# Zeros late in the plan, routing buffers in an early pool, a fifth half of weights in the place of q and k, twelve raw chunks ahead

## The chip, the core and the metric

The kernel runs on one core of one Trainium2 chip. Its engines are PE (matrix products), DVE (the vector engine), ACT (the scalar engine), POOL (GpSimd) and SP (the engine that here only issues transfers); 16 DMA engines move data between device memory and the on-chip memory. The metric is the device time of one execution in microseconds.

## What is computed

Attention with two kinds of heads, then a mixture of experts in which every expert keeps at most 80 tokens. Shapes: q, k, v are 8 x 8 x 576 x 64; 4608 tokens of 512 features; 8 experts with w1 512 x 1024 and w2 1024 x 512, all float32.

```python
mask_local   = (rel >= 0) & (rel < 32)                   # heads 0 to 3
mask_strided = (rel >= 0) & (key % 32 == query % 32)     # heads 4 to 7
attn = softmax(where(mask, q @ k.T / 8, -1e9)) @ v
x = attn.transpose(0, 2, 1, 3).reshape(4608, 512)
logits = x @ w_gate; expert = argmax(logits); gate_w = max of softmax(logits)
out = zeros
for e in range(8):
    tok = tokens of expert e; if more than 80, the 80 with the largest gate_w
    out[tok] = gate_w[tok] * (relu(x[tok] @ w1[e]) @ w2[e])
```

Of the 4608 rows of the output at most 640 are not zero, so all of it is first written with zeros (18 transfers of 512 KB) and the experts' rows are scattered over them at the end.

## The kernel before

It has three stages.

**The plan** (attention and gates). The operations of eight batches are put into a list (`pn.op`). The class `Plan` gives each of them an engine and a place by a simulation with fixed costs; PE keeps the order in which the list was made, the others take what is ready, the most urgent first. `rank` is a due time and `at` an earliest time in the simulation; a transfer with a rank is only taken there when little is under way. What comes out is only an order for each engine: on the chip each engine runs its list in that order and waits where a semaphore says so. SP's list holds all loads and stores: per batch q and k in two parts each (L402, L404), v in two layouts (`vz`, L413, and `vs`, L424), stores of the attention's rows to `xs` in device memory (L563, L566, L703), and, woven in by `weights()` and `zeros()`, the chunks of weights (L289) and the zeros (L887).

**Weights.** An expert has two halves, w1 and w2; the order of the 16 halves is in `halves` (w1 of expert 0, w1 of 1, w2 of 0, w1 of 2, ...). A half is four chunks of 512 KB. Each chunk is split into two 16-bit parts, `hi` by ACT (L303, in the plan L877 in two pieces) and `lo` by DVE (L304, in the plan L879), and the halves live in eight buffers `spl0` to `spl7`. `NPRE` halves (4 before) are loaded and split within the plan, through two staging buffers (`ring`). Five chunks more are loaded raw in the plan, three right after it: eight raw chunks in `slots`, made of `ring`, `raw` (where q and k land) and `kst` (keys of the strided heads; its other part is the source of the zeros).

**The transition** (L977 on). The last gates are turned; DVE finds the 16 largest of each segment (`max`, `max_index`), counts ranks (L1025, L1037), a product makes the table of tokens (L1064), DVE reads it (`idx`, L1073) and POOL gathers the 80 rows of each of the first four experts from `xs` (`xg`, L1078). The buffers of this stage are in the pool `rt`, which is made after the pool `ap` of the attention is closed, and lies where `ap` lay: the first write of `rt` waits for the last use of what lay there, which includes the last store to `xs` (L703, out of `vz`).

**The experts.** For every half `weave` puts the matrix products, `splits` (as many chunks as `BSPL` says, 3, 3, 4 in turn), `xprep` (turning of the gathered rows, L1124) and `finish` (L1187, scaling and scatter) into one order by the fractions in `WIN`. Each `wsplit` also asks for the load of the chunk eight further on, into the slot that it frees. After down products ACT empties PSUM (`yab`, L947), POOL adds two parts (`y`, L1179), PE turns them (`yt`, L1187).

Names in the profile: `spl<-ring`, `spl<-raw`, `spl<-kst` are splits out of these staging buffers; `out<-kst` is a transfer of zeros; `xs<-vz` the last store of attention rows.

Of the kernel before, what the change touches and what calls it, by code (L numbers as in the profile page):

```python
# [193 lines left out]
def moe_attention(ctx: ExitStack, tc, q, k, v, wg, w1, w2, cap, out):  # L194
    nc = tc.nc
# [71 lines left out]
    halves = [(0, 0)]
# [5 lines left out]
        return spls[h] if h < NPRE else (spls[NPRE:] + spls[:NPRE])[(h - NPRE) % len(spls)]  # L273

    def stage(i):
        i0 = NCH * NPRE
        return ring[i % NR] if i < i0 else slots[(i - i0) % NST]

    def wload(i):

# [8 lines left out]
        nc.sync.dma_start(dst, src)  # L289

    def wsplit(pool=False):

# [4 lines left out]
        hi, lo = s_[:, 0, CH * c:CH * c + CH], s_[:, 1, CH * c:CH * c + CH]
        if pool:
            nc.gpsimd.tensor_scalar(r, r, SC, 0.0, op0=ALU.mult, op1=ALU.add)
            nc.scalar.copy(hi, r)  # L300
            nc.gpsimd.tensor_tensor(lo, r, hi, op=ALU.subtract)
        else:
            nc.scalar.activation(hi, r, AF.Copy, scale=SC)  # L303
            nc.vector.scalar_tensor_tensor(lo, r, SC, hi, op0=ALU.mult, op1=ALU.subtract)  # L304
# [558 lines left out]

    def weights():
        i0 = NCH * NPRE
        for i in range(i0 + 5):
            wk = [("ring", i % NR)] if i < i0 + NR else [rawk[0]] if i == i0 + 2 else \
                ["kst0", "kst1"] + [("qk", 1, 1, m, x) for m in range(2) for x in range(2)]
            t = W0 + WSTEP * i
            add(sy(), lambda e, i=i: wload(i), w=wk, kb=524, at=t, rank=t + 8.0)  # L870
            if i < i0:
                r, s_ = ring[i % NR], spls[i // NCH]
                c = i % NCH
                hi, lo = s_[:, 0, CH * c:CH * c + CH], s_[:, 1, CH * c:CH * c + CH]
                for m in range(WSPL):
                    sl = slice(CH // WSPL * m, CH // WSPL * (m + 1))
                    add(dict(A=ac(CH // WSPL)), lambda e, hi=hi, r=r, sl=sl: nc.scalar.activation(  # L877
                        hi[:, sl], r[:, sl], AF.Copy, scale=SC), r=wk, w=[("hi", i, m)], rank=t + 12.0 + WSTEP)
                    add(dict(V=ve(CH // WSPL)), lambda e, lo=lo, hi=hi, r=r, sl=sl: nc.vector.scalar_tensor_tensor(  # L879
                        lo[:, sl], r[:, sl], SC, hi[:, sl], op0=ALU.mult, op1=ALU.subtract),  # L880
                        r=wk + [("hi", i, m)], rank=t + 13.0 + WSTEP)

    def zeros():
        add(sy(), lambda e: nc.sync.dma_start(xs[0:1], zrow[0][0:1, 0:512]), r=["kst0"], kb=2, slow=5.0, rank=60.0)
        for i in range(18):
# [1 line left out]
            add(sy(), lambda e, i=i, x=x: nc.sync.dma_start(  # L887
                outv[i], zrow[x].unsqueeze(1).broadcast_to([64, 2, 1024])), r=["kst%d" % x], kb=524,
                at=Z0 + ZSTEP * i, rank=Z0 + ZSTEP * i + 15.0)
# [98 lines left out]
    nc.vector.max_index(ci[:, 8:16], cv[:, 8:16], gv2)
# [34 lines left out]
    nc.vector.tensor_scalar(pos.rearrange("p a b -> p (a b)"), cv, 0.0, None, op0=ALU.is_gt)
# [48 lines left out]
    with nc.allow_low_precision("token ids are integers"):  # L1072
        nc.vector.tensor_reduce(idx, tab[:, :, 0:2], op=ALU.add, axis=AX.X)  # L1073
    NX = 4
    xg = [rt.tile([SLOTS, DM], F32, name=f"xg{i}") for i in range(NX)]

    def gather(e):
        nc.gpsimd.indirect_dma_start(out=xg[e % NX], out_offset=None, in_=xs[:, :],  # L1078
# [268 lines left out]
```

## Time and profile before

| | |
|---|---|
| median of 3 runs | 333.69 us (333.15 to 335.94) |
| the profiled execution | 331.08 us |
| its span, first to last instruction | 329.4 us |
| mean granted PE clock | 0.895 |
| busy: PE, DVE, ACT, POOL | 264.4, 227.5, 205.0, 121.0 us |
| moved by DMA | 85.34 MB, 259 GB/s over the span |

The plan runs to about 227 us of the span, the transition to about 247 us, the experts to about 323 us; the rest is the last scatter and the program's end. In the profile's rows "L12" is line 12 of the kernel before, times are microseconds unless marked ns, and the part in brackets at a row's end says how long the engine was idle ahead of it and what ended that. Matrix products are pipelined, so a busy PE need not be at its peak.

### The profile page before, as it was taken

How to read it: one execution, taken by the hardware profiler on the slowest of the kernel's cores; microseconds unless marked ns; L12 is line 12 of the kernel's file. 1: busy time of each engine (PE TensorE's matmuls, PEld its weight loads, DVE VectorE, ACT ScalarE, POOL GpSimd, SP SyncE). 2: the span in 40 equal slices, each digit the busy share in tenths (PEclk: the TensorE clock that was granted, in tenths of full speed). 3: DMA queues.
4: the chain of work that ended last, by engine and by line, in shares of the span. 5: the costliest groups of instructions: out<-in, count | busy, mean ns of one | idle time of the engine just before them, and what ended most of it. 6: DMA issues, size and time to landing. Idle time of an engine off the chain costs nothing. (4 is left out here: it accounts for less than half of the span.)

```text
span 329.4 us, 11542 instructions
## 1 busy us (share of the span) xinstructions
PE 264.4 (80%) x4927; PEld 232.7 (71%) x4927; DVE 227.5 (69%) x443; ACT 205.0 (62%) x325; POOL 121.0 (37%) x148
## 2 busy tenths in 40 slices
PE   5765897989978996996998996967058999699791
PEld 5554786778767795885877785746058999599670
DVE  5882766576952977664686766444757999999920
ACT  1574687569775784673668674352207998999810
POOL 8981384271062353162162270000563152322231
PEclk9997698999997997898799799897676999799987
DMA  7978797999997999999796899953537999999401
GB/s 250 247 224 265 208 354 291 166 400 332 253 278 286 217 243 385 183 254 348 202 325 266 193 319 305 259 153 76 189 107 256 347 372 389 401 401 387 169 23 42
DMA packets 56456, 85.34 MB, mean 259 GB/s; under 512 B 23125, under 2 KB 32341, under 8 KB 56402
## 3 DMA queue, kind: packets, MB, share of 16 engines
q1 hardware_dynamic: 54482, 80.79, 79.5%
q0 software_dynamic: 1920, 3.79, 3.5%
q8 instruction: 40, 0.66, 0.8%
q14 instruction: 14, 0.11, 0.1%
HBM read 63.21 MB, written 20.19 MB: 253 GB/s over the span
## 5 line engine op out<-in xcount | busy, mean ns | idle before, releaser
L419 POOL TENSOR_SCALAR vz<-vz 32x1088 f32<-32x1088 f32 x32 | 36.3, 1136 | 44.2 <-DMA vz<-v 37.8
L1132 PE MATMUL hp<-xe,spl 128*128 128x80 f16 x256 | 32.1, 209 | 0.5 <-ACT xe L1126 0.5
L304 DVE SCALAR_TENSOR_TENSOR spl<-raw,spl 128x1024 f16<-128x1024 f32 x24 | 31.8, 1353 | 0.9 <-ACT spl L303 0.9
L1133 PE MATMUL hp<-xe,spl 128*128 128x80 f16 x256 | 32.0, 209 | 0.3 <-DVE xe L1127 0.3
L1134 PE MATMUL hp<-xe,spl 128*128 128x80 f16 x256 | 32.0, 209 | 0.0
L879 DVE SCALAR_TENSOR_TENSOR spl<-ring,spl 128x512 f16<-128x512 f32 x32 | 26.4, 842 | 7.9 <-ACT spl L877 7.8
L672 PE MATMUL pb<-ptm,vs 72*64 72x72 f32 x512 | 22.4, 257 | 9.7 <-DMA ptm<-ptu 4.4
L532 PE MATMUL pb<-vz,ptl 128*32 128x130 f32 x576 | 25.7, 353 | 4.1 <-ACT ptl L364 4.1
L672 PEld LDWEIGHTS pb<-ptm,vs 72*64 72x64 f32 x512 | 21.0, 162 | 11.0 <-DVE rs L626 3.4
L1133 PEld LDWEIGHTS <-spl 128*128 128x128 f16 x256 | 26.9, 105 | 0.9 <-issue 0.7
L445 POOL TENSOR_SCALAR cp<-raw 128x1152 f32<-128x1152 f32 x13 | 16.1, 1235 | 31.1 <-DMA raw<-k 17.8
L1134 PEld LDWEIGHTS <-spl 128*128 128x128 f16 x256 | 26.8, 105 | 0.4 <-issue 0.4
L1132 PEld LDWEIGHTS <-spl 128*128 128x128 f16 x256 | 26.9, 105 | 0.0
L1169 PE MATMUL yp<-he,spl 128*128 128x160 f16 x224 | 26.9, 243 | 0.0
L532 PEld LDWEIGHTS pb<-vz,ptl 128*32 128x32 f32 x576 | 21.9, 145 | 6.6 <-ACT ptl L364 4.3
L303 ACT ACTIVATE spl<-raw 128x1024 f16<-128x1024 f32 x24 | 24.9, 1055 | 2.5 <-DMA raw<-moe_w 1.9
L1168 PE MATMUL yp<-he,spl 128*128 128x80 f16 x196 | 25.0, 206 | 0.0
L465 PE MATMUL pb<-ident,cp 128*128 128x128 f32 x144 | 20.2, 297 | 5.7 <-DVE cp L445 2.9
L610 PE MATMUL pb<-kst,qs 128*18 128x36 f32 x1024 | 20.0, 252 | 3.4 <-issue 3.4
L465 PEld LDWEIGHTS pb<-ident,cp 128*128 128x128 f32 x144 | 17.3, 151 | 7.2 <-ACT pl L510 3.2
L610 PEld LDWEIGHTS pb<-kst,qs 128*18 128x18 f32 x1024 | 18.3, 122 | 5.7 <-issue 5.7
L364 ACT COPY kst<-pb 64x512 f32<-64x512 f32 (+1 forms) x30 | 21.1, 705 | 1.0 <-DVE kst L366 0.5
(207 smaller groups left out, 708.7 us busy)
## 6 DMA issues: line engine op xcount, KB each, us to landing
ring<-moe_w SPq DMA_DIRECT2D x28, 512.0 KB
raw<-moe_w SPq DMA_DIRECT2D x24, 512.0 KB
raw<-q SPq DMA_DIRECT2D x16, 576.0 KB
raw<-k SPq DMA_DIRECT2D x16, 576.0 KB
out<-kst SPq DMA_DIRECT2D x18, 512.0 KB
kst<-moe_w SPq DMA_DIRECT2D x12, 512.0 KB
vs<-v SPq DMA_DIRECT2D x8, 576.0 KB
vz<-v SPq DMA_DIRECT2D x16, 288.0 KB
```

The costliest lines, as they stand in the source:

```text
L304: nc.vector.scalar_tensor_tensor(lo, r, SC, hi, op0=ALU.mult, op1=ALU.subtract)
L419: nc.gpsimd.tensor_scalar(vz[64 * u:64 * u + 32, h, 1:NTL, u, 0:D], vz[64 * u + 32:64 * u + 64, h, 0:NTL - 1, u, 0:D], 1.0, 0.0, op0=ALU.m ...
L465: nc.tensor.transpose(ps(t, P * (j - a), P * (j - a) + P), src[:, j], ident)
L532: nc.tensor.matmul(ps(t, 512 * k_ + 130 * i, 512 * k_ + 130 * i + 130)[32 * g:32 * g + 32], ptl[:, c, 32 * g:32 * g + 32], vz[:, h, tt, :, ...
L610: nc.tensor.matmul(so[32 * h:32 * h + 18, :, :, z], qs[:, h, r::16], kst[:, :, h, r::16], start=False, stop=(g % 2 == 1 and z == 3), tile_ ...
L672: nc.tensor.matmul(o[64 * x:64 * x + 64, :, h], vs[:, h, 2 * g + x], ptm[:, :, 2 * g + x, h], start=True, stop=True)
L879: add(dict(V=ve(CH // WSPL)), lambda e, lo=lo, hi=hi, r=r, sl=sl: nc.vector.scalar_tensor_tensor(lo[:, sl], r[:, sl], SC, hi[:, sl], op0=A ...
L1132: nc.tensor.matmul(o, w[:, 0, i:i + P], x[:, 0, c], start=first, stop=False)
L1133: nc.tensor.matmul(o, w[:, 0, i:i + P], x[:, 1, c], start=False, stop=False)
L1134: nc.tensor.matmul(o, w[:, 1, i:i + P], x[:, 0, c], start=False, stop=last)
L1168: nc.tensor.matmul(ab[:, 0], w[:, 1, i:i + P], he[:, 0, c], start=False, stop=False)
L1169: nc.tensor.matmul(ab, w[:, 0, i:i + P], he[:, :, c], start=(c == 0), stop=(c == 7))
```

## The change

Four things are changed together, and the numbers of the plan with them.

- **Zeros.** Their earliest time goes from `26 + 8 i` to `150 + 1.5 i` and their due time from 15 to 200 behind that; the plan then puts them late and behind the weights.
- **Routing buffers.** `pl`, `pr`, `ptl` and `ptu` move from the pool `ap` into a pool `ae` ahead of it. `rt` therefore lies over `ae`; the gathered rows `xg` get a pool `rt2` of their own behind it, and `scr` is one row instead of eight.
- **A fifth half.** `NPRE` is 5. The fifth half's buffer is part of a new tile `eb`, in which the attention's `qt`, `qs` and `ktl` also lie; so its four chunks (16 to 19) are split once the last scores have been read.
- **Twelve raw chunks.** Behind the 20 split chunks, 12 are loaded raw: four into `ring` and `raw`, four into the last buffer of halves (`far_`, free until half 7), four more into `raw` and `kst`. From then on a split asks again for the chunk eight further on.

In the experts 44 chunks are split instead of 48; `RS` moves one split ahead of the first `xprep`, `BSPL` spreads the rest over more halves, and `finish` comes a little later.

```diff
-NPRE = 4
-NPOST = 4
+NPRE = 5
+NPOST = 3
...
-    slots = (ring + [raw[:, 0:CH]] + [kstt[:, CH * j:CH * j + CH] for j in range(2)] +
-             [raw[:, CH * j:CH * j + CH] for j in range(1, 4)])
+    slots = ring + [raw[:, CH * j:CH * j + CH] for j in range(4)] + [kstt[:, CH * j:CH * j + CH] for j in range(2)]
...
-    spls = [wpool.tile([P, 2, HALF], F16, name=f"spl{i}") for i in range(NPRE)]
+    eb = wpool.tile([P, 8 * S + 128], F32, name="eb")
+    spls = [wpool.tile([P, 2, HALF], F16, name=f"spl{i}") for i in range(NPRE - 1)]
+    spls.append(eb[:, 0:HALF].bitcast(F16).rearrange("p (a f) -> p a f", a=2))
...
     def stage(i):
-        i0 = NCH * NPRE
-        return ring[i % NR] if i < i0 else slots[(i - i0) % NST]
+        k = i - NCH * NPRE
+        if k < 0:
+            return ring[i % NR]
+        if 4 <= k < 8:
+            return far_[k - 4]
+        return slots[k if k < 4 else (k - 8 + 4) % NST if k < 12 else (k - 12) % NST]
...
-        j = i + (NR if i < NCH * NPRE else NST)
-        if j < NCHUNKS:
+        k = i - NCH * NPRE
+        j = i + (12 if k < 4 else NST)
+        if j < NCHUNKS and not 4 <= k < 8:
             late.append(lambda: wload(j))
...
+    ae = actx.enter_context(tc.tile_pool(name="ae", bufs=1))
     ap = actx.enter_context(tc.tile_pool(name="ap", bufs=1))
...
-    pl = ap.tile([P, 9, P], F32, name="pl")
+    qt = eb[:, 0:2 * S].rearrange("p (h s) -> p h s", h=2)
+    qs = eb[:, 2 * S:4 * S].rearrange("p (h s) -> p h s", h=4)
+    ktl = eb[:, 4 * S:8 * S + 128].rearrange("p (h u s) -> p h u s", h=2, u=2)
+    pl = ae.tile([P, 9, P], F32, name="pl")
...
     flush()
-    for j in range(NR + 3, NST):
-        wload(NCH * NPRE + j)
+    wload(NCH * NPRE + 9)
     warm(WARM_[0])
     actx.close()
     rt = wctx.enter_context(tc.tile_pool(name="rt", bufs=1))
+    rt2 = wctx.enter_context(tc.tile_pool(name="rt2", bufs=1))
     wpool3 = wctx.enter_context(tc.tile_pool(name="wpool3", bufs=1))
     spls += [wpool3.tile([P, 2, HALF], F16, name=f"spl{i}") for i in range(NPRE, NPRE + NPOST)]
+    fl = spls[-1].rearrange("p a f -> p (a f)").bitcast(F32)
+    far_ += [fl[:, CH * j:CH * j + CH] for j in range(4)]
+    for j in list(range(4, 8)) + [10, 11]:
+        wload(NCH * NPRE + j)
...
-    xg = [rt.tile([SLOTS, DM], F32, name=f"xg{i}") for i in range(NX)]
+    xg = [rt2.tile([SLOTS, DM], F32, name=f"xg{i}") for i in range(NX)]
...
-Z0 = 26.0
-ZSTEP = 8.0
+Z0 = 150.0
+ZSTEP = 1.5
+ZR = 200.0
-BSPL = [3, 3, 4]
+BSPL = [3, 2, 3, 3]
-RS = 1
+RS = 2
```

What the plan makes of the new numbers on SP, from the last but one store of the strided heads' rows on (L703 before, L711 now). Before:

```order
L703 DMA xs<-xn 576x1x256
L424 DMA vs<-v 72x4x512
L289 DMA kst<-moe_w 128x2x512
L563 DMA xs<-xl 128x4x256
L566 DMA xs<-xl 64x256
L289 DMA kst<-moe_w 128x1024
L703 DMA xs<-xn 576x1x256
L703 DMA xs<-vz 576x1x256
L289 DMA raw<-moe_w 128x1024 x3
```

And of the changed kernel, where `spl_3152` is the last buffer of halves, used as staging:

```order
L574 DMA xs<-xl 64x256
L295 DMA raw<-moe_w 128x1024
L711 DMA xs<-xn 576x1x256
L898 DMA out<-kst 128x1x1024
L295 DMA raw<-moe_w 128x1024
L295 DMA ring_122<-moe_w 128x1024
L295 DMA ring_123<-moe_w 128x1024
L898 DMA out<-kst 128x1x1024
L295 DMA raw<-moe_w 128x1024
L711 DMA xs<-vz 576x1x256
L898 DMA out<-kst 128x1x1024 x6
L295 DMA raw<-moe_w 128x1024
```

Six transfers now stand between the last two stores to `xs`, where there was none, and behind `xs<-vz` come six zeros and then seven chunks (the one shown, four into `spl_3152` and two into `kst`) instead of three. Ten more zeros stand a batch or two earlier, four and six in a row.

On DVE, the end of the plan, around the logits of the last batch (`lg`), before:

```order
L758 RECIPROCAL mm<-mm 96x6
L759 TENSOR_TENSOR gates<-eq,mm 96x48
L735 TENSOR_REDUCE lg<-pb 96x48
L743 TENSOR_REDUCE mm<-lg 96x6
L744 TENSOR_TENSOR ex<-lg,mm 96x48
L749 TENSOR_TENSOR eq<-lg,mm 96x48
```

And now:

```order
L767 TENSOR_TENSOR gates<-eq,mm 96x48
L890 SCALAR_TENSOR_TENSOR eb<-ring_122,eb 128x512 x2
L743 TENSOR_REDUCE lg<-pb 96x48
L890 SCALAR_TENSOR_TENSOR eb<-ring_123,eb 128x512
L751 TENSOR_REDUCE mm<-lg 96x6
L752 TENSOR_TENSOR ex<-lg,mm 96x48
L890 SCALAR_TENSOR_TENSOR eb<-ring_123,eb 128x512
L757 TENSOR_TENSOR eq<-lg,mm 96x48
```

Four half splits of chunks 18 and 19 have come among the steps of the last gates; four others, of chunks 16 and 17, stand a little ahead. On ACT their four `hi` parts stand the same way around the emptying of the last logits.

The first write of a routing buffer on DVE, with the semaphores that it waits for (DMAHW are those of SP's transfers, DMASW those of POOL's), before:

```order
L979 MAX msk<-msk 128x8 [waits DVE_49]
L982 TENSOR_TENSOR wgt<-msk,segm 128x256 [waits DVE_49]
L987 MAX_INDEX msk<-msk,g_117 128x8
L988 MAX_INDEX msk<-msk 128x8
L1023 TENSOR_SCALAR pos<-msk 128x16 [waits DMAHW0_49,DMASW7_49,DMAHW1_49,DMASW6_49,DMAHW2_49,DMASW5_49,DMAHW3_49,DMASW4_49,DMAHW4_49,DMASW2_49,DMAHW5_49,DMASW1_49,DMAHW6_49,DMASW0_49,DMAHW7_49,Activation_49,Pool_49]
```

And now:

```order
L990 MAX msk<-msk 128x8 [waits DVE_49]
L993 TENSOR_TENSOR wgt<-msk,segm 128x256 [waits DVE_49]
L998 MAX_INDEX msk<-msk,g_117 128x8
L999 MAX_INDEX msk<-msk 128x8
L1038 TENSOR_SCALAR pos<-msk 128x16 [waits DMASW4_49,DMASW5_49,DMASW2_49,DMASW6_49,DMASW1_49,DMASW7_49,DMASW0_49,Pool_49]
```

The wait for SP's transfers, the last store among them, has left this row; what is left are POOL's transfers of `ptm`, whose last user is a batch earlier. The first gather and the first split in `spl5` now wait for SP's stores to `xs` instead.

More of the change, by code (lines that the diff above doesn't have):

```diff
@@ L326, in moe_attention @@
     cps = [ap.tile([P, 9, P], F32, name=f"cp{i}") for i in range(2)]
-    qt = ap.tile([P, 2, S], F32, name="qt")
-    qs = ap.tile([P, 4, S // 2], F32, name="qs")
-    ktl = ap.tile([P, 2, 2, 32 + S], F32, name="ktl")
-    pl = ap.tile([P, 9, P], F32, name="pl")
-    pr = ap.tile([P, 8, 18, 4], F32, name="pr")
-    ptl = ap.tile([P, 9, P], F32, name="ptl")
-    ptu = ap.tile([72, 8, 4, 18], F32, name="ptu")
+    qt = eb[:, 0:2 * S].rearrange("p (h s) -> p h s", h=2)
+    qs = eb[:, 2 * S:4 * S].rearrange("p (h s) -> p h s", h=4)
+    ktl = eb[:, 4 * S:8 * S + 128].rearrange("p (h u s) -> p h u s", h=2, u=2)
+    pl = ae.tile([P, 9, P], F32, name="pl")
+    pr = ae.tile([P, 8, 18, 4], F32, name="pr")
+    ptl = ae.tile([P, 9, P], F32, name="ptl")
+    ptu = ae.tile([72, 8, 4, 18], F32, name="ptu")
     ptm = ap.tile([72, 4, 8, 4, 18], F32, name="ptm")
@@ L865, in weights @@
         i0 = NCH * NPRE
[L866 to L869, printed above, removed]
+        eb_ = [("qk", g, w, m, x) for g in range(2) for w in range(2) for m in range(2) for x in range(w + 1)]
+        add(dict(V=0.01), lambda e: None, w=eb_ + ["eb"])
+        places = [[("ring", 0)], [("ring", 1)], [rawk[0]], [rawk[0], rawk[1]], [rawk[1], rawk[2]]]
+        for i in list(range(i0 + 4)) + [i0 + 8]:
+            wk = [("ring", i % NR)] if i < i0 else places[i - i0 if i < i0 + 4 else 4]
+            t = W0 + WSTEP * i if i < i0 + 4 else W0 + WSTEP * (i0 + 4)
             add(sy(), lambda e, i=i: wload(i), w=wk, kb=524, at=t, rank=t + 8.0)
@@ L874, in weights @@
                 hi, lo = s_[:, 0, CH * c:CH * c + CH], s_[:, 1, CH * c:CH * c + CH]
+                ek = ["eb"] if i >= NCH * (NPRE - 1) else []
                 for m in range(WSPL):
@@ L877, in weights @@
                     add(dict(A=ac(CH // WSPL)), lambda e, hi=hi, r=r, sl=sl: nc.scalar.activation(
-                        hi[:, sl], r[:, sl], AF.Copy, scale=SC), r=wk, w=[("hi", i, m)], rank=t + 12.0 + WSTEP)
+                        hi[:, sl], r[:, sl], AF.Copy, scale=SC), r=wk + ek, w=[("hi", i, m)], rank=t + 12.0 + WSTEP)
                     add(dict(V=ve(CH // WSPL)), lambda e, lo=lo, hi=hi, r=r, sl=sl: nc.vector.scalar_tensor_tensor(
                         lo[:, sl], r[:, sl], SC, hi[:, sl], op0=ALU.mult, op1=ALU.subtract),
-                        r=wk + [("hi", i, m)], rank=t + 13.0 + WSTEP)
+                        r=wk + ek + [("hi", i, m)], rank=t + 13.0 + WSTEP)
     def zeros():
@@ L888, in zeros @@
                 outv[i], zrow[x].unsqueeze(1).broadcast_to([64, 2, 1024])), r=["kst%d" % x], kb=524,
-                at=Z0 + ZSTEP * i, rank=Z0 + ZSTEP * i + 15.0)
+                at=Z0 + ZSTEP * i, rank=Z0 + ZSTEP * i + ZR)
     load(0, 0, 0)
@@ L1017, in moe_attention @@
                      esel.unsqueeze(1).unsqueeze(3).broadcast_to([P, NCAND, E, 5]), op=ALU.mult)
-    scr = rt.tile([P, 8, NSEG * NCAND], BF16, name="scr")
+    scr = rt.tile([P, NSEG * NCAND], BF16, name="scr")
     rank = rt.tile([P, 8], F32, name="rank")
@@ L1024, in moe_attention @@
     for m in range(3):
-        nc.vector.tensor_scalar(scr[:, m], call, cv[:, 4 * m + 3:4 * m + 4], None, op0=ALU.is_gt, op1=ALU.add,
+        nc.vector.tensor_scalar(scr, call, cv[:, 4 * m + 3:4 * m + 4], None, op0=ALU.is_gt, op1=ALU.add,
                                 accum_out=rank[:, m:m + 1])
@@ L1036, in moe_attention @@
     for m in range(4):
-        nc.vector.tensor_scalar(scr[:, 3 + m], call, thr[:, m:m + 1], None, op0=ALU.is_gt, op1=ALU.add,
+        nc.vector.tensor_scalar(scr, call, thr[:, m:m + 1], None, op0=ALU.is_gt, op1=ALU.add,
                                 accum_out=rank[:, 3 + m:4 + m])
@@ L1308 @@
 W0 = 14.0
-WSTEP = 8.5
+WSTEP = 8.0
 WSPL = 2
-Z0 = 26.0
-ZSTEP = 8.0
+Z0 = 150.0
+ZSTEP = 1.5
+ZR = 200.0
 BPOOL = []
-BSPL = [3, 3, 4]
+BSPL = [3, 2, 3, 3]
 WARM = 40
 WARM_ = [48, 0, 32, 0]
-RS = 1
+RS = 2
 EV = dict(y="a", ys="a")
-WIN = dict(b=(0.2, 1), bx=(0.12, 0.55), bf=(0.78, 0.92), bl=(0.3, 0.4))
+WIN = dict(b=(0.2, 1), bx=(0.12, 0.55), bf=(0.8, 0.94), bl=(0.3, 0.4))
 FILL = dict(l=0, s=0, q=0, r=0)
```

1 line of the change is left out of this document (added).

## The prediction

> **What bounds the kernel now.** I first cut the execution into stages: busy time of each engine, granted clock, DMA share and GB/s.
>
> ```profile
> span 329.4 us, 11542 instructions
> 80.00:155.00 75.00, 63.91 (x1284) 55.72 (x1280) 50.02 (x110) 49.70 (x84) 27.89 (x31) 0.93 1.00 273
> 155.00:205.00 50.00, 44.24 (x886) 37.85 (x884) 34.71 (x77) 33.14 (x59) 16.28 (x18) 0.90 0.89 270
> 205.00:227.00 22.00, 17.79 (x256) 14.15 (x252) 11.22 (x44) 9.77 (x19) 0.00 (x0) 0.84 0.57 166
> 227.00:247.00 20.00, 7.49 (x97) 6.96 (x95) 11.36 (x42) 2.00 (x2) 9.20 (x17) 0.73 0.50 152
> 247.00:323.00 76.00, 68.53 (x1300) 64.72 (x1298) 66.23 (x70) 61.75 (x85) 21.84 (x19) 0.91 0.82 300
> ```
>
> The columns are PE, PE weight load, DVE, ACT, POOL. The middle of the plan has DMA full (1.00) and PE with holes; from 205 us DMA is half idle, and in the transition everything is. In the experts PE and DVE are both near 90%, so there it must be asked who waits for whom.
>
> The transition by its timeline (start, duration, engine, idle before):
>
> ```profile
> 226.27 0.45 DVE L988 FIND_INDEX8 msk<-msk 128x8 uint32<-128x288 f32 x1
> 226.79 0.58 SPq L703 DMA_DIRECT2D xs<-vz  x1
> 231.73 2.00 ACT L303 ACTIVATE spl<-ring 128x1024 f16<-128x1024 f32 x2 [5.00 <-DMA xs<-vz]
> 231.89 0.17 DVE L1023 TENSOR_SCALAR pos<-msk 128x16 f32<-128x16 f32 x1 [5.16 <-DMA raw<-moe_w]
> 240.68 0.17 DVE L1073 TENSOR_REDUCE idx<-pb 80x8 int32<-80x16 f32 x1 [0.82 <-PE pb L1064]
> 241.14 1.82 POOL L1078 DMA_INDIRECT xg<-xs,idx  x1 [4.08 <-DVE idx L1073]
> 246.68 0.63 PE L1124 MATMUL xp<-ident,xg 80*128 80x80 f32 x3 [2.89 <-DMA xg<-xs,idx]
> ```
>
> DVE has its indices at 226.72 and may write the first routing buffer only at 231.89. The row blames `raw<-moe_w`, but the buffer lay where `vz` was, and ACT, with the same wait, names the store `xs<-vz`: 4.94 us from its issue to ACT's release. Everything to the first turning at 246.68 hangs on it.
>
> The experts: DVE's groups in 247 to 323, PE's total wait there, and the chain of one such wait.
>
> ```profile
> L304 DVE SCALAR_TENSOR_TENSOR spl<-raw,spl 128x1024 f16<-128x1024 f32 x24 | 31.8, 1353 | 0.9 <-ACT spl L303 0.9
> L304 DVE SCALAR_TENSOR_TENSOR spl<-kst,spl 128x1024 f16<-128x1024 f32 x12 | 14.2, 1211 | 0.0
> L304 DVE SCALAR_TENSOR_TENSOR spl<-ring,spl 128x1024 f16<-128x1024 f32 x10 | 12.5, 1277 | 0.0
> PE yt L1187 <- POOL y L1179: 6.4, 4, 3.2
> 280.36 1.06 ACT L303 ACTIVATE spl<-raw 128x1024 f16<-128x1024 f32 x1 [0.29 <-DMA raw<-moe_w]
> 281.32 0.67 ACT L947 COPY yab<-yp 128x640 f32<-128x640 f32 x1
> 282.07 1.75 POOL L1179 TENSOR_TENSOR y<-yab 128x320 f32<-128x320 f32 x1 [4.23 <-ACT yab L947]
> 283.88 0.89 PE L1187 MATMUL yt<-ident,y 128*80 128x128 f32 x4 [3.21 <-POOL y L1179]
> 247.00:255.00 8.00, 7.18 (x120) 6.87 (x119) 6.07 (x8) 6.32 (x10) 2.72 (x3) 0.60 0.79 255
> 284.00:287.50 3.50, 3.50 (x38) 3.42 (x38) 3.50 (x5) 3.25 (x5) 1.07 (x1) 0.52 1.03 395
> 309.00:311.40 2.40, 0.34 (x3) 0.34 (x4) 2.40 (x3) 2.17 (x4) 1.04 (x1) 1.00 0.02 7
> 311.40:314.80 3.40, 3.40 (x39) 3.33 (x38) 3.40 (x5) 1.12 (x2) 1.20 (x1) 0.50 0.08 22
> ```
>
> ACT, late with its splits, empties `yab` late, POOL adds late, and PE stands 3.21 us; after that its clock is 0.52 for 3.5 us. The same comes again around 311, and the stage begins at 0.60. So the experts run at the pace of the splits, on DVE (66.23 of 76) and behind it ACT and DMA; PE pays for their lag twice, in the gap and in the clock.
>
> The Trainium skill, "TensorE: Matmul & The Clock Gate", section "Why this matters for your kernels", warns of PE gaps above about 3 us; here 2.4 us before 311.4 was enough for a clock of 0.50, by the rule that window would run at full clock and 1.7 us less be to gain. I count every such gap with its clock.
>
> **The change, part by part.** All against the profiled execution, 331.08 us, which is 2.6 us below the median of 333.69; I add that at the end.
>
> *Routing buffers: -5.2.* The first routing write loses the wait for SP's transfers, so 5.16 us go. What is late next is the gather, which needs `xs<-vz` landed, and `idx`. Today the store is released at 231.73 and `idx` would come at 240.68 - 5.16 = 235.5, so 3.8 us of room are left for a store delayed by the transfers now ahead of it. Two zeros and four chunks are put between the last two stores: 6 x 0.524 = 3.1 MB, about 8 us at the 395 GB/s above, where DMA is 0.57 busy in 22 us and so idle for 9.5. I take the room as enough.
>
> *The gather itself: +1.* Now it runs beside six zeros and seven chunks.
>
> ```profile
> DMA to landing us min/median/max: 4.6/5.6/7.7
> ```
>
> These are the eight gathers of today, those amid full DMA among them. The first took 246.68 - 241.14 = 5.5. From 0 to +2.2; I take +1.
>
> *The fifth half: +1.6.* Eight half splits on DVE and eight on ACT join the end of the plan.
>
> ```profile
> L879 DVE SCALAR_TENSOR_TENSOR spl<-ring,spl 128x512 f16<-128x512 f32 x2 | 1.4, 681 | 0.0
> 209.72 0.18 DVE L541 TENSOR_SCALAR rs<-pb 128x18 f32<-128x18 f32 x1 [6.20 <-PE pb L532]
> 219.59 0.40 ACT L364 COPY raw<-pb 128x288 f32<-128x288 f32 x1 [0.87 <-PE pb L718]
> 220.65 0.35 DVE L735 TENSOR_REDUCE lg<-pb 96x48 f32<-96x192 f32 x1 [3.72 <-PE pb L730]
> ```
>
> The first four on DVE (2.7 us) lie in its hole of 6.20 us. Two of the last four lie in the hole of 3.72; the other two stand between the steps of the last gates and cost 2 x 0.68. Ahead of `raw` ACT has 0.87 us for two pieces of some 0.5 each (half of the two whole splits in 2.00 above), +0.2. Sum 1.6; from 0.7 to 5 if the load of chunk 18 or 19 is late, since ACT and DVE then stand before the last logits and PE waits for those.
>
> *Zeros out of the early plan: -3.* Of the 18 zeros only those of the first row below are issued in 155 to 205 today, so eleven leave the time before that, 5.8 MB, of which two more chunks take back 1.0. At the 273 GB/s of the stage that is 17 us of DMA time where DMA is full. What PE would gain is bounded by its gaps there:
>
> ```profile
> out<-kst SPq DMA_DIRECT2D x7, 512.0 KB
> POOL vz L419 <- DMA vz<-v: 37.8, 6, 12.1
> 100.14 0.34 PE L610 MATMUL pb<-kst,qs 128*18 128x36 f32 x8 [3.37 <-issue]
> 128.27 0.99 PE L672 MATMUL pb<-ptm,vs 72*64 72x72 f32 x12 [3.26 <-DVE rs L626]
> ```
>
> If the clock follows as it does in the experts, some 5 us per gap. POOL's 12.1 us for one load of v shows the queue; but neither PE row names DMA. From 0 to -12; I take -3. The late part pays: 18 zeros instead of 7 fall behind 155 us, but eight of them into idle DMA behind 213 us. I count this at 0 to +6, and take 0.
>
> *What a zero costs: as much as a chunk.* A zero is read from 64 partitions. Three zeros and two chunks, issued in turn,
>
> ```profile
> 166.37 0.68 SPq L887 DMA_DIRECT2D out<-kst  x1
> 170.05 1.11 SPq L887 DMA_DIRECT2D out<-kst  x1
> 171.00:177.40 6.40, 6.34 (x163) 5.69 (x162) 4.62 (x14) 5.71 (x11) 3.17 (x5) 1.00 1.04 409
> ```
>
> moved at 409 GB/s; 5 x 0.524 MB take 6.4 us at that, 1.3 each. No row shows several zeros alone, which could be slower; that is rival A. The Trainium skill speaks for A: "SBUF — State Buffer", sections "Door 1: The DMA port swizzle" and "Can I just issue two DMAs to hit both halves?", gives a transfer of 64 partitions half of the ports, 196 GB/s, and hardly any overlap to two on opposite halves, by which a zero would take an estimated 2.7 us. For zeros among chunks the row disagrees.
>
> *The experts: -8.* DVE loses five of the 46 splits behind the first turning (four chunks are split earlier, one moves ahead of it): 5 x 1.21 = 6.1, leaving some 60 of its 66.23. PE's own need:
>
> ```profile
> 265.39 0.53 PE L1187 MATMUL yt<-ident,y 128*80 128x128 f32 x3 [0.35 <-POOL y L1179]
> 272.96 0.50 PE L1187 MATMUL yt<-ident,y 128*80 128x128 f32 x3
> 321.73 1.03 PE L1158 MATMUL yt<-spl,he 128*80 128x512 f16 x4
> ```
>
> One expert without a gap takes 272.96 - 265.39 = 7.57. From 246.68 to 322.76 it has 76.1 us; the two gaps (3.2, 2.4) and half of the two slow windows (1.7 each) make 9.0, and the 3.2 lost at 0.60 in the first 8 us stay. So PE needs about 67 and DVE about 62 with its start: at best -9, at worst, if the splits stay the pace and only their sum shrinks, -6, or -4 if late chunks go on holding ACT up (the 0.29 above). DMA follows: twelve raw chunks are there or on the way at the start, and 32 at 0.524 MB and 395 GB/s need 42 us. I take -8 (-4 to -9).
>
> Sum: -5.2 + 1 + 1.6 - 3 + 0 - 8 = -13.6; 331.08 - 13.6 = 317.5, and on the scale of the median **320 us**.
>
> **Rivals.**
>
> *A: zeros in a row cost double*, because their 64 partitions keep half of the DMA engines idle when no chunk runs beside them: 2.6 us each. Six take 16 us instead of 8, so the seven chunks behind `xs<-vz` and the gather's rows come some 8 us later; about half is hidden behind the transition and the four chunks already there: +5, and the late plan +3. 328. For it: its zeros stand in rows of four and six; against it: the 409 GB/s. 0.18.
>
> *B: the late plan stalls, slower.* DMA is the bound behind 155 us, and loads of v for the last two batches stand behind four and six zeros in SP's one queue. Nine transfers more by balance there: 4.7 MB at the 270 GB/s of that stage, 17 us, all paid; the experts stay at DMA's pace; only the routing gains: 333.7 + 17 + 1.6 - 5.2 = 347. It decides where a load of v lands over 10 us behind its issue, near the 12.1 above. Against it: DMA is 0.57 in 205 to 227, which takes half, giving some 339. 0.07.
>
> *C: the early plan gains in full:* the two gaps and their clocks go, and shorter waits with them, -12 instead of -3: 311. For it: 1.00 of DMA there. Against: no PE row names DMA. 0.12.
>
> *D: one of the parts does nothing* (the gap behind `y` stays, or the gather eats the routing's gain): 326. 0.08.
>
> **The numbers.** Forecast 0.55, on its own 315 to 328: the terms' likelier bounds are +-3 on the plan, +-1 on the gather, -1 and +4 on the experts. 1% (3.3 us) is what a measurement of this kernel can tell. Below 330.4: 0.54 of the forecast, C, 0.07 of D and 0.11 of A: 0.84. Within 1%: 0.07 of A and 0.01 of each of the forecast, D and B: 0.10. Slower: 0.06. The range reaches from C to A: 311 to 330.
>
> **What would show it.** The first routing write within 0.5 us of the last index search; the first turning about 5 us earlier against the plan's end; the eight `eb` splits without long waits; DMA near 0.9 or less in 80 to 155, and near 1 from 205 on; no PE gap above 1 us behind `y`, and a clock of 1.00 through the experts. I am wrong if ACT or DVE wait for `ring` before the last logits, if PE's gaps behind 155 us grow, or if the gather lands over 8 us behind its issue.

## The result, and the profile after

The changed kernel takes 322.80 us (median of 4 runs, 320.56 to 325.84) against 334.81 (4 runs, 333.15 to 337.67): a ratio of 0.961, 95% interval 0.950 to 0.972. The profiled execution fell from 331.08 to 323.60 us, its span from 329.4 to 321.9. The stages of the changed kernel, with the columns PE, PE weight load, DVE, ACT, POOL, clock, DMA share, GB/s:

```profile
80.00:155.00 75.00, 66.31 (x1291) 56.05 (x1288) 50.42 (x112) 49.26 (x85) 25.23 (x29) 0.91 0.91 245
227.00:247.00 20.00, 10.18 (x130) 9.35 (x129) 13.19 (x44) 4.33 (x5) 9.19 (x12) 0.76 1.01 310
243.20:314.10 70.90, 65.41 (x1300) 61.10 (x1300) 61.08 (x65) 56.12 (x80) 22.92 (x18) 0.97 0.89 315
```

DMA fell from 1.00 to 0.91 in the early plan and rose from 0.50 to 1.01 in the transition. The last row is the experts, from the first turning to the last `ys`: 70.9 us at a clock of 0.97, where they had 76.1 at 0.91. The transition by its timeline:

```profile
225.66 0.45 DVE L999 FIND_INDEX8 msk<-msk 128x8 uint32<-128x288 f32 x1
226.03 0.15 DVE L1038 TENSOR_SCALAR pos<-msk 128x16 f32<-128x16 f32 x1
227.17 10.03 SPq L898 DMA_DIRECT2D out<-kst  x6
231.81 2.00 ACT L309 ACTIVATE spl<-ring 128x1024 f16<-128x1024 f32 x2 [5.69 <-DMA xs<-vz]
235.29 2.13 POOL L1093 DMA_INDIRECT xg<-xs,idx  x1 [4.99 <-DMA out<-kst]
243.23 0.77 PE L1139 MATMUL xp<-ident,xg 80*128 80x80 f32 x4 [5.21 <-DMA xg<-xs,idx]
248.76 1.06 ACT L309 ACTIVATE spl<-spl 128x1024 f16<-128x1024 f32 x1 [3.34 <-DMA spl<-moe_w]
```

The first routing write follows the last index search at once (it stood 5.16 us). The gather is issued 5.85 us earlier but takes 7.94 us to the first turning instead of 5.54. Behind that ACT stands 3.34 us for a far chunk (`spl<-moe_w`), which was loaded behind the six zeros that SP issued for 10 us.

All profiled executions of the study, cut at the same places (us; "last search" is the start of the second index search, "to write" the time from there to the first routing write, "gather" from its issue to the first turning, "experts" from that to the last `ys`). The ratios leave out executions more than 1.5% above the fastest of their kernel; where the column is empty, too few are left.

| kernel | profiled | last search | to write | gather | experts | ratio to before, 95% |
|---|---|---|---|---|---|---|
| before | 331.08 | 226.27 | 5.62 | 5.54 | 76.16 | 1 |
| before, again | 335.64 | 230.65 | 5.63 | 5.31 | 75.13 | |
| before, routing buffers alone | 330.50 | 232.40 | 0.36 | 5.66 | 74.73 | |
| after | 323.60 | 225.66 | 0.37 | 7.94 | 70.84 | 0.961 (0.950 to 0.972) |
| after, again | 323.08 | 225.45 | 0.37 | 6.36 | 73.25 | |
| routing over the plan | 328.23 | 225.36 | 7.38 | 8.72 | 68.21 | 0.990 (0.983 to 0.996) |
| zeros early | 322.27 | 226.74 | 0.37 | 8.51 | 68.39 | 0.969 (0.958 to 0.980) |
| zeros behind the far chunks | 320.63 | 223.83 | 0.37 | 9.18 | 69.59 | 0.965 (0.956 to 0.974) |
| old weave | 329.27 | 225.89 | 0.37 | 6.10 | 79.66 | 0.988 (0.972 to 1.004) |
| zeros early, old weave | 327.48 | 226.50 | 0.37 | 8.48 | 74.74 | 0.975 (0.964 to 0.986) |
| the same, four halves | 326.84 | 225.15 | 0.37 | 8.08 | 75.55 | 0.986 (0.977 to 0.994) |
| four halves, new weave | 343.08 | 231.96 | 0.37 | 9.50 | 83.79 | 1.021 (1.005 to 1.038) |
| zeros early, kst first | 324.12 | 229.43 | 0.37 | 8.43 | 67.42 | 0.965 (0.958 to 0.973) |
| six early, kst first | 320.50 | 225.90 | 0.37 | 8.81 | 67.28 | 0.968 (0.961 to 0.975) |

One kernel's plan ends up to 4.4 us apart in two executions (226.27 and 230.65), and an interval is 0.6 to 1.6% to either side; what follows is read stage by stage, and a difference of totals below 1% is not read at all. The mean of the two profiled executions of each kernel: plan 228.5 to 225.6, -2.9; first write -5.25; gather +1.7; experts 75.65 to 72.05, -3.6; the rest under 0.2. Sum -10.0, as 333.36 to 323.34.

### The profile page after: what moved, and what is told of

Read it like the earlier page. It is cut to its first block, busy times and chain, and to the rows that moved or that the text cites. A ratio compares the mean times of both kernels' runs of the same rounds, so it can differ in the third digit from the quotient of the medians.

```text
span 321.9 us, 11566 instructions
## 1 busy us (share of the span) xinstructions
PE 263.3 (82%) x4927; PEld 229.4 (71%) x4927; DVE 228.0 (71%) x449; ACT 203.5 (63%) x328; POOL 121.0 (38%) x147
## 3 DMA queue, kind: packets, MB, share of 16 engines
HBM read 63.21 MB, written 20.19 MB: 259 GB/s over the span
## 5 line engine op out<-in xcount | busy, mean ns | idle before, releaser
L372 ACT COPY eb<-pb 128x640 f32<-128x640 f32 (+3 forms) x52 | 36.1, 729 | 31.0 <-PE pb L473 27.8
L1148 PE MATMUL hp<-xe,spl 128*128 128x80 f16 x256 | 30.6, 205 | 1.4 <-DVE xe L1142 1.4
L1147 PE MATMUL hp<-xe,spl 128*128 128x80 f16 x256 | 30.8, 205 | 0.6 <-ACT xe L1141 0.5
L890 DVE SCALAR_TENSOR_TENSOR spl<-ring,spl 128x512 f16<-128x512 f32 x32 | 24.6, 798 | 9.1 <-ACT spl L888 9.0
L1149 PE MATMUL hp<-xe,spl 128*128 128x80 f16 x256 | 30.6, 205 | 0.5 <-DVE spl L310 0.5
L1149 PEld LDWEIGHTS <-spl 128*128 128x128 f16 x256 | 26.0, 102 | 2.3 <-issue 1.7
L1148 PEld LDWEIGHTS <-spl 128*128 128x128 f16 x256 | 26.0, 102 | 0.9 <-issue 0.9
L1147 PEld LDWEIGHTS <-spl 128*128 128x128 f16 x256 | 26.0, 102 | 0.0
L540 PEld LDWEIGHTS pb<-vz,ptl 128*32 128x32 f32 x576 | 20.5, 137 | 5.4 <-ACT ptl L372 3.5
L310 DVE SCALAR_TENSOR_TENSOR spl<-raw,spl 128x1024 f16<-128x1024 f32 x18 | 23.4, 1327 | 0.5 <-ACT spl L309 0.5
L888 ACT ACTIVATE spl<-ring 128x512 f16<-128x512 f32 x32 | 18.2, 621 | 8.4 <-DMA ring<-moe_w 8.4
L500 PE MATMUL pb<-eb 128*32 128x128 f32 x576 | 20.7, 307 | 1.3 <-ACT eb L372 1.3
L500 PEld LDWEIGHTS pb<-eb 128*32 128x32 f32 x576 | 18.5, 124 | 4.4 <-issue 2.5
L618 PE MATMUL pb<-kst,eb 128*18 128x36 f32 x1024 | 20.0, 251 | 1.6 <-issue 1.6
```

Of the source, the lines that this page charges most:

```text
L372: nc.scalar.copy(o, i)
L500: nc.tensor.matmul(ps(t, P * c, P * c + P)[32 * g:32 * g + 32], qt[:, h, 32 * tt:32 * tt + 32], ktl[:, h, :, 32 * tt:32 * tt + 64], start= ...
L540: nc.tensor.matmul(ps(t, 512 * k_ + 130 * i, 512 * k_ + 130 * i + 130)[32 * g:32 * g + 32], ptl[:, c, 32 * g:32 * g + 32], vz[:, h, tt, :, ...
L618: nc.tensor.matmul(so[32 * h:32 * h + 18, :, :, z], qs[:, h, r::16], kst[:, :, h, r::16], start=False, stop=(g % 2 == 1 and z == 3), tile_ ...
L1147: nc.tensor.matmul(o, w[:, 0, i:i + P], x[:, 0, c], start=first, stop=False)
L1148: nc.tensor.matmul(o, w[:, 0, i:i + P], x[:, 1, c], start=False, stop=False)
```

## The experiments

**The two kernels again.** Nothing is edited.

> The changed kernel once more beside the other runs of this chip, as the measure for them: about 0.96 of the kernel before by every theory.

> The kernel before, profiled a second time, since its first profiled execution (331.08 us) lay below all its others and the changed kernel's did not. Theory, the terms are differences of stages and repeat: last index search at 226 us, 14.4 us from it to the store's release, idx and the first turning at 20 behind it, experts 76 us. Rival, the first execution was a lucky one in a stage whose part I then mis-sized: a stage (the experts with their gaps behind y, or the plan) is 3 to 5 us longer.

The changed kernel, measured together with the two runs on the zeros and with `routing over the plan`: median 325.99 (4 runs, 319.68 to 329.26), 323.08 profiled; the kernel before there 336.08 (14 runs). The kernel before, second profile:

```profile
230.65 0.45 DVE L988 FIND_INDEX8 msk<-msk 128x8 uint32<-128x288 f32 x1
236.28 0.17 DVE L1023 TENSOR_SCALAR pos<-msk 128x16 f32<-128x16 f32 x1 [5.18 <-DMA raw<-moe_w]
250.84 0.77 PE L1124 MATMUL xp<-ident,xg 80*128 80x80 f32 x4 [2.92 <-DMA xg<-xs,idx]
```

From the last search to the first turning 20.19 us, the first time 20.41; the experts 75.1 and 76.2. What differs is the plan, by 4.4 us. So the first profiled execution was low by its plan, and the stages behind it repeat to about 1 us.

**The routing buffers, alone and taken back.** In the kernel before, the early pool `ae` for `pl`, `pr`, `ptl`, `ptu`, the pool `rt2` for `xg` and one row of `scr`; in the changed kernel, the order of the two early pools turned round:

```
-    ae = actx.enter_context(tc.tile_pool(name="ae", bufs=1))
     ap = actx.enter_context(tc.tile_pool(name="ap", bufs=1))
+    ae = actx.enter_context(tc.tile_pool(name="ae", bufs=1))
```

> The kernel before with the routing buffers' part of the change alone: pl, pr, ptl and ptu in an early pool of their own, xg in a second late pool, one row of scr. Theory (term of -5.2): the first routing write comes within 0.5 us of the last index search, the first turning 5 us earlier, and as the experts run at the pace of the splits, the splits' start must move with it: between 3 and 5 us less than before. Rival, the experts are held by the chunks, whatever the time of the first turning: the stage grows by what the routing saves, and the time falls by under 1.5 us.

> The changed kernel with the two early pools in the old order, so that the routing buffers lie over vz again; all else as changed, the six zeros behind the last store too. Theory (term of -5.2): the first routing write waits again until SP's store of vz has landed, some 5.5 us behind the last index search, and the time is 5 us longer than the changed kernel's. Rival: the wait was only exchanged for a longer gather (7.9 us instead of 5.5) and for late chunks, so that with a later gather both come back: the first turning is only some 2.5 us later and the time 1 to 3 us longer. Rival that the plan's end sets it: no difference.

The timeline of the first, and then of the second:

```profile
232.40 0.45 DVE L989 FIND_INDEX8 msk<-msk 128x8 uint32<-128x288 f32 x1
232.76 0.15 DVE L1025 TENSOR_SCALAR pos<-msk 128x16 f32<-128x16 f32 x1
247.44 0.77 PE L1126 MATMUL xp<-ident,xg 80*128 80x80 f32 x4 [3.04 <-DMA xg<-xs,idx]
```

```profile
225.36 0.45 DVE L999 FIND_INDEX8 msk<-msk 128x8 uint32<-128x288 f32 x1
232.74 0.17 DVE L1038 TENSOR_SCALAR pos<-msk 128x16 f32<-128x16 f32 x1 [6.92 <-DMA out<-kst]
250.76 0.77 PE L1139 MATMUL xp<-ident,xg 80*128 80x80 f32 x4 [6.29 <-DMA xg<-xs,idx]
```

Alone, the stretch from the last search to the first turning falls from 20.2 to 15.04 us, the experts do not grow (74.73), and the profiled time is 5.1 us below that of the second profile of before, though the plan ended 1.75 us later. (Its ten timed runs lie between 323.82 and 337.44, median 333.18 against 335.38, too far apart for an interval; what it is worth in the total is therefore open, and the stages alone are read.) Taken back, the wait is there again at 6.92 us, longer than before: the store, with six zeros behind it, now takes 6.76 us from its issue to ACT's release (4.94 before); the first turning comes 7.5 us later than in the first profile of the changed kernel, the experts are 2.6 us shorter, since the far chunks are there by then (ACT waits 0.5 us for chunks), and the profiled time is 4.6 us longer; the ratio is 0.990 (0.983 to 0.996) where the changed kernel has 0.961 (0.950 to 0.972). The term of -5.2 stands, and the rival by which the stage behind eats it falls for the kernel before; for the changed kernel it was right in part.

**The zeros.** Early again (Z0 = 26, ZSTEP = 8, ZR = 15); and twelve in the plan, the last six in the code behind the far chunks:

```
-    for j in list(range(4, 8)) + [10, 11]:
+    for j in range(4, 8):
+        wload(NCH * NPRE + j)
+    for i in range(12, 18):
+        nc.sync.dma_start(outv[i], zrow[i % 2].unsqueeze(1).broadcast_to([64, 2, 1024]))
+    for j in (10, 11):
         wload(NCH * NPRE + j)
```

> The changed kernel with the old due times of the 18 zeros (26, step 8, urgency 15): they stand in the plan up to about 200 us and none behind the last store. Theory (terms -3 and 0): DMA is full again in 80 to 155 us and the plan ends about 3 us later, while the gather lands in 5.5 us instead of 7.9 and the chunks behind it wait for no zeros, 2 to 4 us back: within 2 us of the changed kernel. Rival, the zeros' move carries the gain: 5 us longer or more. Rival, the zeros do harm where they are now and nothing early: 3 us shorter, with the plan's end where it is.

> The changed kernel with the six zeros that stand between the last store and the far chunks issued behind the four far chunks instead, ahead of the two into kst. Theory, the chunks stand behind the zeros (a piece of rival A): ACT's and DVE's waits for the far chunks at 249 to 256 us (3.3 and 2.3 on ACT, 3.2 and 1.8 on DVE) go, the experts are 3 us shorter, and the gather stays at some 8 us. Rival, the zeros only move: the chunks into kst come 8 us later and ACT waits for those: no difference. Rival, the late chunks are the price of the whole DMA being full, whoever stands ahead: waits spread over later chunks, within 1 us.

ACT's largest row of waits for chunks in the experts (in total, how many, the longest), first in the changed kernel, then with the zeros early, then behind the far chunks:

```profile
ACT spl L309 <- DMA spl<-moe_w: 6.1, 3, 3.3
```

```profile
ACT spl L309 <- DMA raw<-moe_w: 1.0, 2, 0.8
```

```profile
ACT spl L309 <- DMA raw<-moe_w: 0.4, 2, 0.2
```

The experts with the zeros early as one window, and the gather and first turning there; then the first turning with the zeros behind:

```profile
244.90:313.30 68.40, 65.78 (x1300) 61.94 (x1300) 61.48 (x65) 56.24 (x80) 21.96 (x18) 0.95 0.76 270
```

```profile
236.37 2.06 POOL L1093 DMA_INDIRECT xg<-xs,idx  x1 [4.99 <-DVE idx L1088]
244.88 0.77 PE L1139 MATMUL xp<-ident,xg 80*128 80x80 f32 x4 [5.98 <-DMA xg<-xs,idx]
```

```profile
242.49 0.77 PE L1143 MATMUL xp<-ident,xg 80*128 80x80 f32 x4 [6.28 <-DMA xg<-xs,idx]
```

In neither is there a wait for `spl<-moe_w`, the far chunks, any more, and the experts then need 68.4 and 69.6 us. So the six zeros cost the stage 1 to 5 us (70.8 and 73.3 less these; in the second profile of the changed kernel the row is 7.0 us), a piece of rival A that the forecast had not priced. Both totals are the changed kernel's within the interval: with the zeros early the plan's end came later (226.74, 226.50 and 229.43 in the three executions with five halves and all zeros early, 227.6 in the mean, against 225.2 in the five with late zeros, 223.83 to 225.89); with the zeros behind, no kernel of the study has a lower median (320.95 of 4 runs), but nothing shows it to beat the changed one. And the gather did not get faster without zeros ahead of it: 8.5 and 9.2 us.

**The weave.** The old numbers in the changed kernel, and the same with the zeros early:

```
-BSPL = [3, 2, 3, 3]
+BSPL = [3, 3, 4]
-RS = 2
+RS = 1
-WIN = dict(b=(0.2, 1), bx=(0.12, 0.55), bf=(0.8, 0.94), bl=(0.3, 0.4))
+WIN = dict(b=(0.2, 1), bx=(0.12, 0.55), bf=(0.78, 0.92), bl=(0.3, 0.4))
```

> The changed kernel with the old numbers of the weave (splits of an expert in groups of 3, 3, 4, one split behind the routing instead of two, the old place of the last group). Theory: a stall of PE behind y of 1 to 3 us comes back in some experts with its slow clock, 0 to 3 us longer. Rival, the splits behind the first turning are what counts and one more of them there costs 1.2 us and no more. Rival that they do nothing: within 0.5 us.

> The changed kernel with the zeros at their old due times and the old numbers of the weave. With the zeros early, no far chunk was late (experts 68.4 us); with the old weave and the zeros late, PE stood 4.61 us behind y at 267.7 us and the experts took 79.7. Theory, the old weave asks for chunks faster than they come, whoever stands ahead of them, and ACT's queue holds y up: a stall behind y and experts of 74 us or more. Rival, the stall came of the late chunks behind the zeros alone: no gap above 1 us, experts 68 to 70 us.

The experts of the first as one window and the 3.5 us behind their longest stall, and that stall by the timeline; then the second's stage and stall:

```profile
241.40:321.00 79.60, 68.88 (x1300) 64.78 (x1300) 60.00 (x66) 57.68 (x80) 25.52 (x19) 0.91 0.82 288
267.70:271.20 3.50, 3.50 (x35) 3.37 (x36) 1.89 (x3) 2.40 (x4) 2.88 (x2) 0.50 1.02 372
```

```profile
261.15 2.35 DVE L310 SCALAR_TENSOR_TENSOR spl<-kst,spl 128x1024 f16<-128x1024 f32 x2
263.42 2.35 DVE L310 SCALAR_TENSOR_TENSOR spl<-ring,spl 128x1024 f16<-128x1024 f32 x2
263.63 4.00 POOL L1194 TENSOR_TENSOR y<-yab 128x320 f32<-128x320 f32 x1 [8.77 <-ACT yab L958]
265.69 1.22 DVE L310 SCALAR_TENSOR_TENSOR spl<-raw,spl 128x1024 f16<-128x1024 f32 x1
266.83 0.48 DVE L1142 SCALAR_TENSOR_TENSOR xe<-xp,xe 128x320 f16<-128x320 f32 x1
267.69 1.07 PE L1202 MATMUL yt<-ident,y 128*80 128x128 f32 x4 [4.61 <-POOL y L1194]
```

```profile
244.50:319.20 74.70, 68.33 (x1300) 64.79 (x1300) 60.72 (x66) 57.73 (x80) 23.93 (x18) 0.90 0.70 248
```

```profile
280.52 3.47 POOL L1194 TENSOR_TENSOR y<-yab 128x320 f32<-128x320 f32 x1 [4.92 <-ACT yab L958]
284.05 1.07 PE L1202 MATMUL yt<-ident,y 128*80 128x128 f32 x4 [5.47 <-POOL y L1194]
```

PE's waits for `y` over the experts (in total, how many, the longest), with the zeros late: the new weave, then the old one. With the zeros early: the new weave; the old one has there the one stall just shown, and the second row is the 3.5 us behind it.

```profile
PE yt L1202 <- POOL y L1194: 1.3, 2, 0.9
PE yt L1202 <- POOL y L1194: 7.4, 4, 4.6
```

```profile
PE yt L1202 <- POOL y L1194: 0.6, 1, 0.6
284.00:287.50 3.50, 3.45 (x34) 3.31 (x35) 1.88 (x3) 2.34 (x4) 0.92 (x1) 0.50 1.03 410
```

The stall behind `y` is back, 4.61 and 5.47 us, with a clock of 0.50 behind each, and the experts take 79.7 and 74.7 us. DVE works 60.0 us of 79.6: it is not the bound. Early zeros do not heal it, so it needs no late chunks; they add to it (79.7 against 74.7). Within the stall the add of POOL itself takes 4.00 us while DVE goes from split to split; the same add takes 0.87 us in the last expert of this execution, where DVE rests. Which of the three numbers does it was not tried apart.

**The fifth half.** NPRE = 4 and NPOST = 4, first with the new weave (a chunk every 9.6 us of the simulated plan), then with the old one and the zeros early (every 8.5 us; 8 with five halves):

> The changed kernel with four halves split in the plan and four behind it (the first three in tiles of their own, the fourth in the place of q and k), chunk loads in the plan spread over the same time, all else as changed. Theory (terms of +1.6 and -8): the plan's end is 1 to 2 us earlier, and the experts, with eight more splits of half a chunk... four whole chunks on DVE and ACT each, 4 x 1.21 = 4.8 us more on DVE, run at the pace of the splits again: 75 us or more instead of 68 to 73, so 3 to 5 us longer than the changed kernel in sum. Rival, the twelve chunks ahead and the weave made the experts faster, not the number of splits: 0 to 1 us shorter.

> The kernel of early_old_weave with four halves split in the plan instead of five, four behind it, the chunks' step in the plan 8.5 as before the change: of the whole change the routing buffers, the places of the buffers and the twelve chunks ahead are left. Against early_old_weave it shows the fifth half alone. Theory (my term of -8: the stage goes by the splits' number): four more splits of 1.21 us on DVE, experts 4 to 6 us longer; the plan's end 0 to 2 us earlier without the eight half splits. Rival, the pace of the weave counts and not the number: experts as long as those of early_old_weave.

The experts with the new weave, and with the old one with its first stall and PE's wait for the last gates (below, the same wait in its partner with five halves):

```profile
251.00:334.80 83.80, 70.09 (x1300) 63.52 (x1300) 66.10 (x69) 60.66 (x83) 23.57 (x18) 0.92 0.76 267
```

```profile
242.80:318.30 75.50, 67.02 (x1300) 63.22 (x1300) 65.60 (x70) 61.62 (x84) 26.99 (x18) 0.93 0.77 273
```

```profile
222.12 0.32 PE L773 MATMUL pb<-ident,gates 96*128 96x96 f32 x1 [2.52 <-DVE gates L767]
263.73 1.07 PE L1202 MATMUL yt<-ident,y 128*80 128x128 f32 x4 [2.55 <-POOL y L1194]
```

```profile
223.36 0.42 PE L773 MATMUL pb<-ident,gates 96*128 96x96 f32 x1 [3.60 <-DVE gates L767]
```

The first does not isolate the fifth half. The new weave hands out 11 splits in four halves; with 20 chunks split in the plan that is enough, with 16 the down products of the last two experts stand in the program ahead of two and three of the splits that they should wait for. Its work is all there, those two experts read some weights unsplit, and its 83.8 us say only that the new weave needs the fifth half. The second does isolate it: four more splits on DVE (65.60 against 60.72 us) make the experts 0.8 us longer (75.5 against 74.7), not 4.8; two executions of one kernel differ by 1.0 and 2.4 there. The plan ends 1.35 us earlier, which alone would be lost in its scatter of 4.4, but 1.08 of it is the wait for the gates, and that repeats: 2.5 us in each profile of the kernel before, 3.6 in each with five halves. It hangs on where the half splits fall: with four halves and the new weave, where they stand among the gates' steps too, it is 3.60, and that plan ended at 231.96. The rival, that the number of splits doesn't count, is right under the old weave. And since this kernel with four halves keeps the twelve chunks ahead and still needs 75.5 us for the experts, as the kernel before does (75.65 in the mean), those chunks gain nothing that shows under the old weave.

**Putting the pieces together.** Zeros early, or six of them early, and the two loads into `kst` ahead of the far ones:

```
-    for j in list(range(4, 8)) + [10, 11]:
+    for j in [10, 11] + list(range(4, 8)):
```

> The changed kernel with the zeros at their old due times, and the two chunks into kst issued ahead of the four far chunks instead of behind them, since kst is then free before the last store has landed and the far chunks' place is not: they use the DMA time of 228 to 232 us. Theory: the gather, which took 8.5 us with six chunks issued just ahead of it, lands some 2 us earlier, and since no chunk is late, the experts (68.4 us, near PE's own need) move with it: 2 us shorter than with the zeros early alone, 318 to 321. Rival, the store of vz lands later beside them, so the far chunks are issued later and ACT waits for them: no gain. Rival, the gather is slow whatever is queued: no gain.

> As kst_first, but with six of the 18 zeros spread over 60 to 130 us and the other twelve late in the plan, so that one zero is left behind the last store. Theory: the plan's end is where that of the late zeros was (225.5 us, against 226.7 with all zeros early), experts 68 to 69 us: 317 to 320. Rival, the plan's end varies by more than the zeros' places move it: no different from kst_first.

Timeline of the first, then the experts of the second:

```profile
231.27 2.16 SPq L295 DMA_DIRECT2D kst<-moe_w  x2
234.98 2.02 SPq L295 DMA_DIRECT2D spl<-moe_w  x4
238.80 2.06 POOL L1093 DMA_INDIRECT xg<-xs,idx  x1 [4.74 <-DMA kst<-moe_w]
247.23 0.77 PE L1139 MATMUL xp<-ident,xg 80*128 80x80 f32 x4 [5.63 <-DMA xg<-xs,idx]
```

```profile
244.10:311.40 67.30, 64.69 (x1300) 60.85 (x1300) 61.32 (x65) 56.13 (x80) 23.16 (x18) 0.97 0.83 292
```

The loads into `kst` went out 3.7 us ahead of the far ones, and the gather still took 8.43 us: it is slow with chunks queued beside it, and nothing here shows that fewer of them help. In these two the experts reach 67.4 and 67.3 us. The totals, 0.965 and 0.968, are the changed kernel's within the interval: the gather takes back part of what the experts gain, and in the first the plan ended 4 us later (229.43). No version shown here beats it.

## Why the prediction was right or wrong

The total, 320 forecast and 322.8 measured, came out of terms some of which were wrong.

*Routing buffers, -5.2: right.* -5.25 in the changed kernel, and -5.3 alone; the room for the store held (ACT was released at 231.81, `idx` came at 234.83).

*The gather, +1: in its range.* +1.7 over the two pairs (7.94 and 6.36 against 5.54 and 5.31), though +2.4 in the first, above the 2.2 allowed. The reason given, zeros and chunks beside it, stands for the chunks: with them queued just ahead it took 8.1 to 9.5 us, with zeros ahead and chunks behind 6.1 to 7.9.

*The fifth half, +1.6: about right;* 1.08 us in the wait for the gates, 1.35 at the plan's end in the one pair that isolates it.

*Zeros, -3 early and 0 late: the first about right, the second wrong.* About -2.3 at the plan's end, by means that one execution's scatter could hide. "I take the room as enough" held for the store, but not for the chunks: SP issued the six zeros at 1.67 us each (10.03 / 6), between my 1.3 and rival A's 2.6, so the far chunks behind them came late, ACT waited 6 to 7 us for them and the experts paid for it. Rival A had the place right and the price too high, and its reason was not seen: in those 10 us the DMA engines were full (1.01, at 335 GB/s). C, a full gain in the early plan, did not come (its share fell to 0.91, the whole plan gained 2.9 us at most); B, the late plan, did not stall.

*The experts, -8: wrong in the size and in its main reason.* -3.6 in the mean of the pairs. The step that failed is "so the experts run at the pace of the splits, on DVE", and with it "five fewer splits x 1.21": four fewer changed the stage by 0.8 us, and with DVE at 60.0 us it took 79.7. The other half of that paragraph held: PE pays for a late `y` in the gap and in the clock, and without gaps needs about 67 us (67.3 to 68.4 measured); no wait behind `y` is above 1 us now (0.9 and 1.0), as forecast. But what took the gaps away were the numbers of the weave, worth 6 to 8 us of stage (zeros late 79.7 against 72.0, zeros early 74.7 against 68.4), and I gave them no term. The forecast size was there to be had: where no chunk is late the stage is 6 to 8 us shorter than the 75.65 before (67.3 to 69.6). That the changed kernel got only 3.6 is the branch that I had priced at -4, late chunks holding ACT up, through other chunks than those of the row that I quoted. The fifth half's use is that it makes the slower weave possible.

*The scale, +2.6: right by luck.* The profiled execution of before was low by its plan, which no term of mine contained, while that of the changed kernel lay 0.8 us above its median; the 2.6 made up for part of what my terms had too much. In the mean of two profiles the sum is -10.0, not -13.6; the plan's part of it (-2.9) may be scatter, and what in the plan's new order it would come from was not settled.

## What to carry to other kernels

A buffer's address can be a wait: let the first writer after a stage lie over what was dead long before, and the time comes back in full when nothing else is late. Where an engine is 87% busy, ask who stands behind it in another engine's queue before counting its work as the pace: here, under the old weave, four fewer splits were worth 0.8 us, and a weave that hands out 33 in twelve halves instead of 40, with its two smaller changes, was worth 6 us of 75. Work moved into idle DMA time is paid by whatever was queued behind it.

## What the runs showed of the hardware

POOL's add of `yab` (128x320) took 0.86 to 0.88 us where DVE rested, 0.9 to 2.0 in most places, and 3.47 to 4.25 us five times, once in each of five executions, all with the old weave. In most places it is a split of DVE that gets longer, as beside the add that starts at 282.07 in the kernel before (1.75 us); a split like this takes 1.21 us elsewhere:

```profile
283.03 1.88 DVE L304 SCALAR_TENSOR_TENSOR spl<-raw,spl 128x1024 f16<-128x1024 f32 x1
```

In the five no split is longer. DVE ran splits without a pause from before the add's start, and the add ended as DVE came from the short `xe` and `he` steps, which read one input from PSUM and last 0.80 us together, to the next split (267.63 above). So the one or the other waits; what decides which was not tested. Of the 4.61 us that PE stood there, about 3.1 are this (4.00 - 0.87). The Trainium skill, "SBUF — State Buffer", section "Who interferes with whom", has DVE and GpSimd share one pair of ports under a lock; the traces agree, and in the five the wait went over more than one DVE instruction.

The first gather's 80 rows took 5.3 to 5.7 us to the first turning with DMA half idle and 8.1 to 9.5 with chunks queued ahead, whether six went just ahead (8.51) or two of them earlier (8.43). Later gathers of the kernel before, beside full DMA (1.01 and 1.05), landed in 6.7 and 7.7 us; with the zeros early two landed in 3.4 and 2.9 us where DMA was nearly idle (0.32 and 0.21). The Trainium skill, "DMA: Bandwidth & Descriptors", section "Queues, rings and completion order", says that a DMA engine takes turns between queues packet by packet, by which the length of the other queue would not matter; 8.51 and 8.43 fit that, but two executions of the changed kernel differ by more (7.94 and 6.36).

A gap of PE of 2.38 us was followed by a clock of 0.50 in the kernel before, one of 2.55 by 0.58 with four halves and the old weave; two others there, of 2.08 and 2.37 us, were followed by 1.00:

```profile
263.70:267.20 3.50, 3.47 (x40) 3.34 (x41) 1.88 (x3) 2.36 (x4) 2.88 (x2) 0.58 0.99 384
290.80:294.30 3.50, 3.49 (x65) 3.48 (x66) 3.50 (x5) 3.49 (x6) 1.32 (x1) 1.00 1.04 394
308.20:311.60 3.40, 3.40 (x65) 3.39 (x66) 3.40 (x4) 1.01 (x2) 1.32 (x1) 1.00 0.00 0
```

The length of the gap alone does not tell.
